# Decoding w_in in sixteen halves of 256 columns instead of eight parts of 512

## The chip, the core and the metric

The kernel runs on one core of a Trainium2 chip. TensorE (PE) multiplies, VectorE (DVE), ScalarE (ACT) and GpSimd (POOL) work on rows of up to 128 partitions, SyncE (SP) only issues transfers. Each engine takes its instructions strictly in the order of its own queue, and waits on semaphores for the other engines.

The metric is the device time of one execution in microseconds, the median of several runs; lower is better.

## The reference

The weights w_in, w_out, w_ch1 and w_ch2 come as 64-bit floats, the rest in single precision. The reference is one attention layer and two feed-forward layers, one behind the other:

```python
scores = scale * q @ k.T          # 4 batches, 8 heads, 576 positions, head width 64, block-causal mask
attn   = softmax(scores) @ v      # -> x: 4 x 576 x 512
h      = relu(x @ w_in)           # w_in: 512 x 1024; u = first half, v = second half
v_n    = (v - mean) / sqrt(var + 1e-6)
v_s    = w_spatial @ v_n + b_spatial
x      = (u * v_s) @ w_out
out    = x + relu(layernorm(x) * g_ln @ w_ch1) @ w_ch2
```

## The kernel before, in words

Attention runs over 16 pairs of heads, and each pair is cut into 9 **units** of query blocks (`UNITS`, line 249): one unit for the 64 rows left over in both heads, then for each head the blocks with 512, 384, 256 and 128 keys. A unit is a matmul of scores on PE, the row maximum and subtraction on DVE (L319), the exponential on ACT (L326), then transposes back on PE (L376), whose results DVE or ACT copies out of PSUM (L368, L370), and at the end of a pair the product with v (L427). The loop of line 557 writes these steps unit by unit; `u` counts the units, so pair p begins at unit 9p.

Matmuls here work on pairs (high, low) of single-precision numbers: `mm3` (L106 to L108) makes three products of them. Who makes such pairs from plain numbers is a `split`: one instruction rounds the value (high), a second subtracts (low). Queries and keys are split into `stack` (rounding on DVE or ACT, L56 and L58; subtraction on POOL, L227, L239, L241); the result of attention is scaled and split into `xT` on POOL (L437, L60, L440).

**w_in** arrives as raw 64-bit words, and `decode` (line 81) makes single-precision numbers of them in three instructions: ACT takes the high words (L88, tile `dm`), DVE shifts the low words (L89, tile `de`), and DVE joins both (L90). The split of w_in is all on POOL: L101 rounds `dm` into `win[0]`, L102 subtracts into `win[1]`. `decode_in` (line 443) does it for eight parts: four row blocks of the columns of v (parts 0 to 3), then four of those of u (parts 4 to 7). Three raw buffers take turns; `fetch(i + 3)` (L450, on the SP queue) loads a part into the buffer of part i once that is decoded. The first product with v's columns is a `value_tile`, the first with u's columns a `gate_unit` (tile `ups`); those of one batch are put in between the attention units of the next.

When the parts are decoded is set by `DECODE` (line 556), a set of units: the first one starts the loads, each further unit decodes one part. L88 and L89 are pinned to that place in the written order (`tc.keep_in_program_order`); all other instructions are put into each engine's order by a scheduler that works with modelled times. The tile `dm` shares a ring of three buffers (`vr`) with the value tiles, `de` a ring of two (`ur`).

Behind attention come the spatial product, w_out and the second feed-forward layer, with their own decodes of 128x256 tiles (`decode_jobs`, line 717); these are not touched.

Of the kernel before, what the change touches and what calls it, by code (L numbers as in the profile page):

```python
# [20 lines left out]
PLAN = {'mm': 3, 'sc': 3, 'tr': 2, 'D': 2, 'hi0': 'v', 'hi1': 's', 'klo0': 'g', 'klo1': 'g', 'qlo0': 'g', 'qlo1': 'g', 'xm0': 'g', 'xm1': 'g', 'xh0': 'g', 'xh1': 'g', 'xl0': 'g', 'xl1': 'g', 'dm': 'g', 'dh': 'g', 'ev0': 3, 'ev1': 2, 'rate': 24500.0, 'vrb': 3, 'ds': 2, 'dy': 1, 'raw': 5, 'yn': 2, 'ts': 3, 'ring': 8, 'wt': 2, 'cb': 1, 'hq': 8, 'packed': 4, 'plain': 3, 'pre': 8, 'py': 10, 'pyn': 4, 'dn0': 2, 'dnn': 5, 'vl': 'v', 'pace': 3, 'wd': 7, 'tl0': 'v', 'tl1': 'v', 'xe': 's', 'pt': 6, 'dstart': 8}  # L21


def f32(ap):
    return ap.bitcast(F32)
# [8 lines left out]
def tile_kernel(  # L34
# [29 lines left out]
    F = w_in.shape[2] // 2  # L64
# [16 lines left out]
    def decode(raw, m, e, out, here=lambda ins: ins):  # L81

        low, high = raw[:, :, 0], raw[:, :, 1]
        here(nc.scalar.activation(m, f32(high), AF.Prelu, scale=2.0**-112, alpha=2.0**32))  # L88
        here(nc.vector.tensor_scalar(e, low, 29, None, op0=ALU.logical_shift_right))  # L89
        nc.vector.scalar_tensor_tensor(  # L90
            out.bitcast(U32), m.bitcast(U32), 3, e, op0=ALU.logical_shift_left, op1=ALU.bitwise_or
        )

    def split(src, hi, lo, high="s", low="g"):

        if high == "s":
            nc.scalar.copy(hi, src)  # L97
        elif high == "v":
            nc.vector.tensor_copy(hi, src)
        else:  # L100
            nc.gpsimd.tensor_scalar(hi, src, 1.0, 0.0, op0=ALU.mult, op1=ALU.add)  # L101
        {"v": nc.vector, "g": nc.gpsimd}[low].tensor_tensor(lo, src, f32(hi), op=ALU.subtract)  # L102
# [29 lines left out]
    win = [xw.tile([128, KD, 2 * F], F32R, name=f"win{i}") for i in range(2)]  # L132
# [310 lines left out]
    def decode_in():  # L443
        raws = {}

        def fetch(i):
            if i < 2 * KD:
                h, kc = 1 - i // KD, i % KD
                raws[i] = dn.tile([128, F, 2], U32, tag="hl", name="raw", bufs=3)
                nc.sync.dma_start(  # L450
                    out=raws[i].rearrange("p a b -> p (a b)"), in_=wi32[:, kc, 2 * F * h:2 * F * h + 2 * F]
                )

        fetch(0)
        fetch(1)
        fetch(2)
        yield
        for i in range(2 * KD):
            h, kc = 1 - i // KD, i % KD
            m = dn.tile([128, F], F32, tag="vr", name="dm", bufs=PLAN["vrb"])  # L460
            e = dn.tile([128, F], U32, tag="ur", name="de")
            cols = slice(F * h, F * h + F)
            decode(raws.pop(i), m, e, m, tc.keep_in_program_order)
            split(m, win[0][:, kc, cols], win[1][:, kc, cols], PLAN['dh'])
            fetch(i + 3)
            yield

    def value_tile(pair, t):

# [54 lines left out]
    dense = None  # L524
    debt = 0.0
    dec = decode_in()
    preps = {}

# [24 lines left out]
    tot = float(sum(size) * NP)  # L553
    D = PLAN['D']
    WARM = {2: 5, 3: 2, 4: 2, 5: 1}
    DECODE = {1, 7, 12, 17, 22, 38, 42, 46, 50}
    for u in range(NS + 8):
        p, i = divmod(u, NU)
        if u < NS:
# [21 lines left out]
        if 0 in preps and i >= 1:  # L581
            next(preps[0], None)
        if u in DECODE:
            next(dec, None)
# [115 lines left out]
    raws = {}  # L700
# [485 lines left out]
```

## Time and profile before

| | us |
|---|---|
| median of 3 runs | 806.68 (804.15 to 809.35) |
| the profiled execution | 802.63 |
| its span in the trace | 800.5 |
| PE busy | 779.9 (97% of the span) |
| DVE, ACT, POOL busy | 528.8, 419.4, 414.4 |

The span is the time from the first to the last instruction in the trace; the time of an execution has 2.1 us more around it. PE is busy nearly throughout, so a change of time has to show as a change of PE's idle time, or as PE's first and last work coming at another time. The busy share of the other engines is a mean: in the attention stage, which takes the first 264 us, POOL is at times as full as PE. PE's granted clock is 1.00 of full speed (2.4 GHz) in every stretch read below.

### The profile page before, as it was taken

Reading aid. Unit: us, or ns where it says so; the run is one execution under the profiler, and the core shown is the slowest. Engines: PE = TensorE matmul, PEld = TensorE weight load, DVE = VectorE, ACT = ScalarE, POOL = GpSimd, SP = SyncE. Lnnn points to the kernel's source line nnn. Section 1 sums busy time; section 2 is a strip of 40 time slices with the busy share of each in tenths; the row PEclk is TensorE's granted clock in tenths of the full one; section 3 lists DMA queues with packets and bytes.
Section 4 is the critical chain, followed back from the end, with each engine's and each line's share of the span. In section 5 each row is a group of like instructions: output and inputs, shape, how many; then the busy total and the mean of one; then the engine's idle time right before and its main releaser. Section 6 shows DMA issues by size and latency. Waiting matters only on the chain.

```text
span 800.5 us, 13287 instructions
## 1 busy us (share of the span) xinstructions
PE 779.9 (97%) x4508; PEld 669.0 (84%) x4508; DVE 528.8 (66%) x1193; ACT 419.4 (52%) x1071; POOL 414.4 (52%) x417
## 2 busy tenths in 40 slices
PE   9989999999999999999999999999999999999998
PEld 4667788778878799889988889888889888888986
DVE  6667855674565277787677787897566588645534
ACT  4777666666755464555354555653354454333421
POOL 4498856754553343223285465465545465545431
PEclk9999999999999999999999999999999999999999
DMA  8855545446141569789420342204001003000002
GB/s 252 198 158 164 149 148 152 131 121 177 68 156 61 152 204 297 214 258 287 150 93 2 106 131 79 80 0 158 1 28 28 0 1 125 21 0 1 1 1 79
DMA packets 53847, 88.70 MB, mean 111 GB/s; under 512 B 6930, under 2 KB 17298, under 8 KB 53780
## 3 DMA queue, kind: packets, MB, share of 16 engines
q1 hardware_dynamic: 53540, 87.55, 36.1%
q8 instruction: 35, 0.57, 0.3%
q10 hardware_dynamic: 240, 0.31, 0.2%
q14 instruction: 32, 0.26, 0.1%
HBM read 68.88 MB, written 18.95 MB: 110 GB/s over the span
## 4 chain that ended last, share of the span: by engine, by line
PE 80%; DVE 6%; DMA 5%; POOL 3%; ACT 2%; issue 2%; SPq 1%; POOLq 0%; ACTq 0%; DVEq 0%
PE hps L965 21%; PE o L106 8%; PE o L108 8%; PE o L107 8%; PE tr L376 5%; PE pv L427 5%; PE sc L304 3%; DMA raw<-in_w_ch_dram 2%; PE ups L106 2%; PE sc L298 2%; PE by L106 2%; PE by L108 2%; PE by L107 2%; PE sc L282 1%; PE ups L108 1%
## 5 line engine op out<-in xcount | busy, mean ns | idle before, releaser
L102 POOL TENSOR_TENSOR a<-s,a 128x256 fp32r<-128x256 f32 x96 | 78.0, 816 | 93.2 <-ACT a L97 93.2
L107 PE MATMUL o<-w,h 128*128 128x512 f32 x288 | 113.0, 394 | 0.0
L106 PE MATMUL o<-w,h 128*128 128x512 f32 x288 | 107.9, 398 | 1.0 <-ACT h L957 1.0
L971 DVE TENSOR_TENSOR c<-hps,c 128x384 f32<-128x384 f32 x120 | 66.5, 554 | 54.8 <-PE hps L965 52.8
L108 PE MATMUL o<-w,h 128*128 128x512 f32 x288 | 97.6, 398 | 0.1
L326 ACT ACTIVATE p<-p,nm 128x512 f32<-128x512 f32 (+3 forms) x128 | 71.2, 557 | 32.0 <-DVE nm L319 26.6
L319 DVE CUSTOM_DVE_ANT_0 p<-sc,mask 128x512 f32<-128x512 f32 (+3 forms) x128 | 58.5, 479 | 40.6 <-PE sc L304 18.9
L102 POOL TENSOR_TENSOR a<-w,a 128x256 fp32r<-128x256 f32 x72 | 61.5, 856 | 44.3 <-ACT a L97 38.6
L97 ACT CAST a<-s 128x256 fp32r<-128x256 f32 x96 | 38.4, 404 | 84.0 <-PE hps L965 75.8
L368 DVE COPY pH<-tr 128x512 f32<-128x512 f32 (+1 forms) x88 | 49.7, 574 | 27.4 <-PE tr L376 26.4
L106 PEld LDWEIGHTS o<-w,h 128*128 128x128 f32 x288 | 53.8, 188 | 11.6 <-ACT h L957 2.3
L107 PEld LDWEIGHTS o<-w,h 128*128 128x128 f32 x288 | 54.2, 188 | 10.1
L108 PEld LDWEIGHTS o<-w,h 128*128 128x128 f32 x288 | 53.2, 188 | 8.8 <-DVE h L958 1.0
L376 PE MATMUL tr<-idn,p 128*128 128x128 f32 x320 | 55.1, 279 | 4.5 <-DVE pH L368 4.4
L815 POOL TENSOR_TENSOR gt<-gf,gt 128x576 fp32r<-128x576 f32 (+1 forms) x17 | 25.5, 1501 | 59.6 <-ACT gt L814 59.6
L239 POOL TENSOR_TENSOR stack<-qkt,stack 64x576 fp32r<-64x576 f32 x24 | 34.7, 1444 | 33.6 <-ACT stack L58 29.3
L376 PEld LDWEIGHTS tr<-idn,p 128*128 128x128 f32 x320 | 37.7, 140 | 14.5 <-DVE pH L368 6.6
L958 DVE SCALAR_TENSOR_TENSOR h<-c,h 128x384 fp32r<-128x384 f32 x72 | 45.9, 657 | 1.5 <-ACT h L957 1.5
L117 POOL TENSOR_TENSOR rs<-rs,nhalf 128x1 f32<-128x1 f32 x36 | 23.3, 649 | 44.9 <-DVE rs L116 44.6
L88 ACT ACTIVATE dm<-raw 128x256 f32<-128x256 f32 (+1 forms) x72 | 31.9, 462 | 27.2 <-DVE w L90 8.0
L437 POOL TENSOR_TENSOR xx<-xx,rb 128x576 f32<-128x576 f32 x16 | 22.7, 1420 | 42.2 <-DMA rb<-r_d 30.1
L304 PE MATMUL sc<-stack 128*128 128x512 f32 (+3 forms) x192 | 43.5, 340 | 0.8 <-DVE nm L319 0.5
(185 smaller groups left out, 2276.7 us busy)
## 6 DMA issues: line engine op xcount, KB each, us to landing
raw<-in_w_ch_dram SPq DMA_DIRECT2D x64, 256.0 KB
qkt<-in_qk_dram SPq DMA_DIRECT2D x110, 144.0 KB
vt<-in_v_dram SPq DMA_DIRECT2D x16, 320.0 KB
rb<-r_d SPq DMA_DIRECT2D x32, 144.0 KB
u_d<-ur SPq DMA_DIRECT2D x16, 288.0 KB
us<-u_d SPq DMA_DIRECT2D x16, 288.0 KB
y_d<-ys SPq DMA_DIRECT2D x18, 256.0 KB
yr<-y_d SPq DMA_DIRECT2D x18, 256.0 KB
```

The costliest lines, as they stand in the source:

```text
L102: {"v": nc.vector, "g": nc.gpsimd}[low].tensor_tensor(lo, src, f32(hi), op=ALU.subtract)
L106: MM(out_ps, lhsT=a[0], rhs=b[0], start=first, stop=False)
L107: MM(out_ps, lhsT=a[0], rhs=b[1], start=False, stop=False)
L108: MM(out_ps, lhsT=a[1], rhs=b[0], start=False, stop=last)
L304: MM(s_ps[:, :nn], lhsT=st[:, j, i, q], rhs=st[:, j, 2, 0:nn], start=(i == 0), stop=(i == 1))
L319: nc.vector.tensor_tensor_reduce(pt[:, o:o + n], s_ps[:, :n], m, -0.125, 3e38, ALU.add, ALU.min, nm[:, i:i + 1])
L326: nc.scalar.activation(pt[:, :n], pt[:, :n], AF.Exp, bias=nm[:, 0:1], scale=-1.0, accum_out=sm[:, col:col + 1])
L368: nc.vector.tensor_copy(out, src)
L376: nc.tensor.transpose(tr[:, o:o + 128], pt[:, 128 * kc:128 * kc + 128], idn)
L958: nc.vector.scalar_tensor_tensor(t[:, 1], src, 0.0, f32(t[:, 0]), op0=ALU.max, op1=ALU.subtract)
L965: MM(ps, lhsT=a[x], rhs=b[y], start=not more and kc == 0 and k == 0, stop=kc == KD // 2 - 1 and k == 2, skip_group_check=True,)
L971: nc.vector.tensor_tensor(out, ps, x, op=ALU.add)
```

## The change

Each part of w_in is decoded and split in two halves of 256 columns. The halves stand at two units in a row (the old unit and the next), the pins on L88 and L89 are put on each half, and the next part is fetched after the second half. The tiles `dm`, `de` and the raw buffer stay one per part.

```diff
-            cols = slice(F * h, F * h + F)
-            decode(raws.pop(i), m, e, m, tc.keep_in_program_order)
-            split(m, win[0][:, kc, cols], win[1][:, kc, cols], PLAN['dh'])
-            fetch(i + 3)
-            yield
+            raw = raws.pop(i)
+            for a in range(0, F, F // 2):
+                part = slice(a, a + F // 2)
+                cols = slice(F * h + a, F * h + a + F // 2)
+                decode(raw[:, part], m[:, part], e[:, part], m[:, part], tc.keep_in_program_order)
+                split(m[:, part], win[0][:, kc, cols], win[1][:, kc, cols], PLAN['dh'])
+                if a:
+                    fetch(i + 3)
+                yield
...
-    DECODE = {1, 7, 12, 17, 22, 38, 42, 46, 50}
+    DECODE = {1} | {u + a for u in (7, 12, 17, 22, 38, 42, 46, 50) for a in range(2)}
```

So there are 8 more instructions on ACT, 16 more on DVE, 16 more on POOL, and as many transfers as before. Beyond about 120 us of the span the order of all engines is what it was. What moved before that is seen at three places.

**Place one: DVE at the end of the third pair** (units 25 and 26 and the next pair's first units; `tail` is the unit of the 64 leftover rows, `sm` its sums, `nm` the row maxima). Before:

```order
L368 COPY pH<-tr 128x4x128
L89 TENSOR_SCALAR de<-raw 128x512
L319 ISA p,nm<-sc,mask 128x128
L319 ISA nm 128x1
L319 ISA tail,nm<-sc,mask 128x256
L319 ISA nm 128x1
L319 ISA tail,nm<-sc,mask 128x320
L319 ISA nm 128x1
L90 SCALAR_TENSOR_TENSOR dm<-dm,de 128x512
L336 TENSOR_SCALAR sm<-sm 128x9
L323 TENSOR_TENSOR nm<-nm 128x1
L319 ISA p,nm<-sc,mask 128x512
```

and with the change:

```order
L368 COPY pH<-tr 128x4x128
L89 TENSOR_SCALAR de<-raw 128x256
L319 ISA p,nm<-sc,mask 128x128
L319 ISA nm 128x1
L319 ISA tail,nm<-sc,mask 128x256
L319 ISA nm 128x1
L319 ISA tail,nm<-sc,mask 128x320
L319 ISA nm 128x1
L90 SCALAR_TENSOR_TENSOR dm<-dm,de 128x256 x2
L323 TENSOR_TENSOR nm<-nm 128x1
L336 TENSOR_SCALAR sm<-sm 128x9
L319 ISA p,nm<-sc,mask 128x512
```

One shift of half the size stands where the whole one stood (its other half went to an earlier place), both joins stand together where one stood, and L323 went ahead of L336.

**Place two: DVE two pairs later** (part 4 and now also the first half of part 5). Before:

```order
L368 COPY pH<-tr 128x2x64
L89 TENSOR_SCALAR de<-raw 128x512
L90 SCALAR_TENSOR_TENSOR dm<-dm,de 128x512
L368 COPY pH<-tr 128x4x128
L319 ISA p,nm<-sc,mask 128x128
L319 ISA nm 128x1
L368 COPY pH<-tr 128x4x128
L319 ISA p,nm<-sc,mask 128x128
L319 ISA nm 128x1
L319 ISA tail,nm<-sc,mask 128x256
```

and with the change:

```order
L368 COPY pH<-tr 128x2x64
L89 TENSOR_SCALAR de<-raw 128x256
L90 SCALAR_TENSOR_TENSOR dm<-dm,de 128x256
L368 COPY pH<-tr 128x4x128
L89 TENSOR_SCALAR de<-raw 128x256
L319 ISA p,nm<-sc,mask 128x128
L319 ISA nm 128x1
L89 TENSOR_SCALAR de<-raw 128x256
L368 COPY pH<-tr 128x4x128
L319 ISA p,nm<-sc,mask 128x128
L319 ISA nm 128x1
L319 ISA tail,nm<-sc,mask 128x256
```

Half the decode stands ahead of the first copy, two more shifts between the first and the second copy; two joins follow behind this piece, ahead of the next row of `tail`.

**Place three: POOL around the last parts** (`rs` belongs to the value tiles, `stack` to a coming pair). Before:

```order
L437 TENSOR_TENSOR xx<-xx,rb 128x576
L117 TENSOR_TENSOR rs<-rs,nhalf 128x1 x2
L60 TENSOR_SCALAR xT_84<-xx 128x576
L440 TENSOR_TENSOR xT_85<-xx,xT_84 128x576
L101 TENSOR_SCALAR win_82<-dm 128x512
L102 TENSOR_TENSOR win_83<-dm,win_82 128x512
L101 TENSOR_SCALAR win_82<-dm 128x512
L102 TENSOR_TENSOR win_83<-dm,win_82 128x512
L239 TENSOR_TENSOR stack_89<-qkt,stack_89 64x576
```

and with the change:

```order
L437 TENSOR_TENSOR xx<-xx,rb 128x576
L101 TENSOR_SCALAR win_82<-dm 128x256
L117 TENSOR_TENSOR rs<-rs,nhalf 128x1 x2
L60 TENSOR_SCALAR xT_84<-xx 128x576
L102 TENSOR_TENSOR win_83<-dm,win_82 128x256
L440 TENSOR_TENSOR xT_85<-xx,xT_84 128x576
L101 TENSOR_SCALAR win_82<-dm 128x256
L102 TENSOR_TENSOR win_83<-dm,win_82 128x256
L101 TENSOR_SCALAR win_82<-dm 128x256 x2
L102 TENSOR_TENSOR win_83<-dm,win_82 128x256 x2
L239 TENSOR_TENSOR stack_89<-qkt,stack_89 64x576
```

Between the last split of `xT` and the next `stack` stood two whole parts; now three halves stand there, and the fourth is put in among the work ahead of them.

## Rows read from the trace of the kernel before

**Rows 1.** By stretch: length, busy us of PE, PEld, DVE, ACT, POOL; clock; DMA.
```profile
20.00:40.00 20.00, 19.41 (x130) 12.82 (x130) 13.81 (x45) 15.65 (x50) 9.98 (x12) 1.00 0.83 198
40.00:53.00 13.00, 11.08 (x81) 7.59 (x81) 10.03 (x30) 9.09 (x26) 12.49 (x12) 1.00 0.49 148
...
69.00:83.00 14.00, 12.65 (x87) 9.82 (x86) 12.06 (x33) 10.04 (x32) 12.71 (x11) 1.00 0.64 189
83.00:105.00 22.00, 20.52 (x139) 16.56 (x138) 16.79 (x49) 15.41 (x38) 18.29 (x17) 1.00 0.42 125
```

**Rows 2.** PE's waits from 20 to 110 us: us in total, times, longest.
```profile
PE tr L376 <- DVE pH L368: 2.8, 5, 1.3
PE tr L376 <- ACT rr L341: 0.9, 1, 0.9
PE sc L298 <- DVE nm L319: 0.9, 1, 0.9
PE rps L339 <- ACT pL L370: 0.8, 1, 0.8
PE sc L304 <- DVE nm L319: 0.5, 1, 0.5
```

**Rows 3.** Chain that ended last, 40 to 106 us: start, us, what.
```profile
44.83 1.29 DVE de L89
...
69.71 1.68 DVE dm L90
...
93.71 1.91 DVE de L89 x2
```

**Rows 4.** POOL in order of time: start, us, instruction.
```profile
44.43 1.40 POOL L239 TENSOR_TENSOR stack<-qkt,stack 64x576 fp32r<-64x576 f32 x1
...
69.33 1.51 POOL L239 TENSOR_TENSOR stack<-qkt,stack 64x576 fp32r<-64x576 f32 x1 [1.84 <-ACT stack L58]
```

**Rows 5.** Groups by line and shape, whole parts: count, busy us, mean ns.
```profile
L90 DVE SCALAR_TENSOR_TENSOR dm<-dm,de 128x512 uint32<-128x512 uint32 x8 | 7.7, 957 | 1.5 <-ACT dm L88 1.4
L89 DVE TENSOR_SCALAR de<-raw 128x512 uint32<-128x512 uint32 x8 | 5.8, 732 | 0.0
L88 ACT ACTIVATE dm<-raw 128x512 f32<-128x512 f32 x8 | 5.3, 666 | 0.9 <-DMA vn_d<-vr 0.9
```

**Rows 6.** Instructions of one line, ns min/median/max, first and last start, shapes.
```profile
L89 DVE TENSOR_SCALAR raw<-raw x68: 276/289/1367, 277.6 to 509.3; 128x256 uint32<-128x256 uint32 x64, 128x512 uint32<-128x512 uint32 x4
L89 DVE TENSOR_SCALAR de<-raw x8: 414/493/1654, 21.3 to 95.2; 128x512 uint32<-128x512 uint32 x8
...
L90 DVE SCALAR_TENSOR_TENSOR w<-dm,raw x32: 405/418/1553, 302.5 to 372.1; 128x256 uint32<-128x256 uint32 x32
L90 DVE SCALAR_TENSOR_TENSOR dm<-dm,de x8: 677/852/1684, 22.8 to 97.0; 128x512 uint32<-128x512 uint32 x8
...
L102 POOL TENSOR_TENSOR a<-s,a x96: 725/739/1495, 401.6 to 773.9; 128x256 fp32r<-128x256 f32 x96
L102 POOL TENSOR_TENSOR win<-dm,win x8: 1266/1279/1578, 24.3 to 99.7; 128x512 fp32r<-128x512 f32 x8
...
L101 POOL TENSOR_SCALAR win<-dm x8: 610/620/627, 23.6 to 99.0; 128x512 fp32r<-128x512 f32 x8
...
L60 POOL TENSOR_SCALAR xT<-xx x16: 661/672/682, 37.7 to 272.5; 128x576 fp32r<-128x576 f32 x16
...
L88 ACT ACTIVATE dm<-raw 128x256 f32<-128x256 f32 x64 | 26.6, 436 | 26.2 <-DVE w L90 8.0 <-DMA raw<-in_w_ch_dram 5.8 <-DVE w2b L90 5.4
```

**Rows 7.** The last split of w_in on POOL, and PE's first product with it, by time.
```profile
99.72 1.28 POOL L102 TENSOR_TENSOR win<-dm,win 128x512 fp32r<-128x512 f32 x1
...
103.25 0.29 PE L108 MATMUL ups<-xT,win 128*128 128x288 f32 x1
```

**Rows 8.** The SP queue's waits from 0 to 110 us: us in total, times, longest.
```profile
SPq L155 <- POOL stack L241: 13.7, 4, 4.6
SPq L450 <- DVE de L89: 3.4, 1, 3.4
```

## The prediction, made before the changed kernel ran

> **What bounds the kernel now.** First the busy times by stretch [rows 1]. PE is the engine to look at: from 40 to 53 us it works 11.08 of 13.00 us, from 69 to 83 us 12.65 of 14.00. These two stretches, where it idles 1.92 and 1.35 us, are not empty elsewhere: POOL is busy 12.49 and 12.71 us there and DVE 10.03 and 12.06, while from 20 to 40 us POOL has half its time free and PE idles only 0.59 us. The clock is at full speed throughout, so what PE loses it loses by waiting.
>
> Then PE's own waits from 20 to 110 us [rows 2]: 5.9 us in nine waits, all for DVE's copies and row maxima or for ACT work that hangs on these. POOL and transfers are not among them. So the question is what makes DVE late. The chain of waits [rows 3] has three long pieces of this very decode in it: the shift L89 at 44.83 us (1.29 us), the join L90 at 69.71 (1.68) and two shifts at 93.71 (1.91).
>
> Then why these are long. A shift of 512 columns takes 414 ns at best and 732 in the mean, a join 677 and 957 [rows 5, 6]. In order of time the long ones lie beside a POOL subtraction: the shift at 44.8 us ends at 46.12, 0.29 us after POOL's L239 that began at 44.43 and took 1.40; the join at 69.71 ends at 71.39, 0.55 us after the one that began at 69.33 and took 1.51 [rows 3, 4]. DVE stood until POOL's instruction was over, and then ran for about its own time. So a decode instruction has two prices: its own time, and the rest of the POOL instruction that it meets. Over the 16 shifts and joins the second price is (732 - 414) x 8 + (957 - 677) x 8 = 4.8 us, 0.30 us each.
>
> **The change part by part.** What is *added* is a fixed cost per instruction, from medians of half-size forms that the later stages run [rows 5, 6]:
> - ACT, 8 more L88: 2 x 436 - 666 = 206 ns a part, 1.6 us.
> - DVE, 16 more: the shift 2 x 289 - 414 = 164 ns, the join 2 x 418 - 677 = 159 ns; 2.6 us.
> - POOL, 16 more: L102 2 x 739 - 1279 = 199 ns. L101 has no row at 256 columns; from 620 ns at 512 and 672 at 576 (L60, the same operation) I take 0.81 ns a column, so 412 ns, an estimate. Its bounds are half of 620 and all of it; the added cost is 0 to 620 ns a part, 204 taken. Together 3.2 us (1.6 to 6.6).
>
> ACT's 1.6 us lie beside idle time: it works 9.09 of 13 and 10.04 of 14 us in the tight stretches. If that cover went, exponentials would come up to 0.2 us later a part. POOL's 3.2 us would be hidden too, since PE waits for no POOL work [rows 2], with one narrow place: the last L102 of w_in ends at 101.00 us, and PE first reads that tile's last row block at 103.25 [rows 7]. That is 2.25 us of cover; with all 3.2 us in front of it PE would wait 1.0 us.
>
> No transfer is added, but each reload of the raw buffer (L450) now waits for the second half, and stands later in the SP queue. Behind it are loads of queries and keys, which on their own wait up to 4.6 us for POOL to free the buffer; L450's worst wait for a shift is 3.4 us [rows 8]. A reload that comes a unit later, some 1.8 us (144 units in the first 264 us), lies inside that. I cost it at nothing; without that cover the loads would be later by those 1.8 us.
>
> What costs time is the *second price* on DVE, which is charged per instruction, not per column. Between 40 and 53 us and from 69 to 83 us, by the order shown, DVE gets five decode instructions more than before: one join at place one; at place two and right behind it two halves of shifts and two of joins. Where POOL is nearly always busy each has to stand again. Bounds for one: nothing beside its own 0.16 us (the shortest of the whole shifts, 414 ns, met nothing), or one whole POOL subtraction, 1.40 us [rows 4]. I take the mean of the rows, 0.30: 5 x (0.16 + 0.30) = 2.3 us. DVE has 2.97 and 1.94 us of idle time in the two stretches, but PE's waits say that it is late at their critical points, so I pass all of it on. From 20 to 40 us DVE has 6.2 us free and the added halves cost nothing.
>
> The SBUF — State Buffer page of the Trainium skill, in "SBUF: two separate sides", says that GpSimd and the DVE instructions that run in a two-port mode or read two inputs from SBUF share a port pair as an exclusive lock: whoever starts first holds it for the whole instruction, and the other fully blocks. The two collisions above agree. By the lock alone each added instruction would meet a busy POOL with the share 12.6 of 13.5 and stand half a subtraction, 0.66 us; five would be 4.1 us instead of 2.3.
>
> What is *gained*: ahead of the copy at 71.39 us for which PE waits now stands a half join, 677 - 418 = 0.26 us shorter, and at 44.8 us a half shift, 414 - 289 = 0.13 us shorter; the pause for the rest of POOL's instruction stays. At place three POOL has three halves between the last `xT` and the next `stack` instead of two parts: 3 x (412 + 739) = 3.45 against 2 x (620 + 1279) = 3.80 us, 0.35 us less on a piece that lies in the chain. Together 0.74 us.
>
> **Sum:** 2.3 - 0.7 = +1.6 us. Against the profiled execution (802.63) that is 804.2; this lies 4.05 us under the median of the runs shown, so against the median the forecast is 806.68 + 1.6 = **808.3 us**, 0.2% slower. The bounds of the second price give 5 x 0.16 - 0.7 = +0.1 and 5 x 1.56 - 0.7 = +7.1.
>
> **The rivals.**
>
> *A gain.* The units of the softmax get in between the halves, and the two worst collisions don't come again. For it: the shift at 44.8 us is followed by a wait of 0.9 us, and the longest wait of PE, 1.3 us, is for the copy behind the join at 69.71 [rows 2, 3]. Against: both halves of the join stand together at place one. If those two waits go and the fixed cost is hidden: -2.2, with place three -2.6: 804.1 us. More is hardly there, since all that PE loses from 20 to 110 us is 5.9 us. This is a chance of 0.22.
>
> *No change.* At place one and at place three halves stand side by side again (two joins, two roundings and two subtractions on POOL), so they are a whole instruction in two pieces. With only the 0.8 us of fixed cost of five DVE instructions against the 0.7 gained: 806.8 us. Chance 0.24.
>
> *Much slower.* DVE gets through one such instruction per POOL instruction: after a block POOL starts its next subtraction at once, and the second half stands for all of that. Its place is the two stretches and the three shifts and three joins around 93 to 98 us, where two and two stood: seven added instructions at 1.56 us, 10.9, less 0.7: 816.9 us. It decides from six whole blocks on (6 x 1.56 - 0.7 = 8.7). For it: the piece at 93.71 us. Against: 0.30 us in the mean, not 1.40. Chance 0.06.
>
> **How the numbers follow.** My forecast, a loss of 0.5 to 7 us, has 0.48. One per cent is 8.1 us, about what a measurement of this kernel can tell from no change (its three runs differ by 5.2). A gain of that size would need more than all waits in the stretch: 0.01. A loss of that size is the third rival: 0.06. Within 1%: 0.93. The range reaches from the gain to the upper bound of the forecast, less a tail on each side: 803.5 to 813 us.
>
> **What the profile would show.** Half shifts near 289 ns at best and joins near 418, with means 0.2 to 0.4 us above; L102 near 739 ns. PE's waits from 20 to 110 us at 6 to 9 us instead of 5.9, again for DVE copies and maxima, at 45 to 53 and 69 to 78 us. The times beyond 120 us shifted as one piece. I am wrong if the means of the halves lie at their best times (then the first rival), if PE waits for POOL's `win` or `stack`, or if it waits more than 0.5 us at places that have no half near them.

## The result, and the profile after

The changed kernel takes 810.15 us in the median of 15 runs (806.93 to 813.35), the kernel before 805.21 in 15 runs beside it: a ratio of 1.0071 with a 95% interval of 1.0056 to 1.0085. It is slower by some 4.9 us, within 1%, as forecast in sign and in range; the forecast's +1.6 us was a third of it.

The head of the page after, with PE's line and the clock line of the 40 slices (tenths of full speed):

```profile
span 809.8 us, 13334 instructions
...
PE 787.4 (97%) x4508; PEld 673.0 (83%) x4508; DVE 532.3 (66%) x1209; ACT 420.3 (52%) x1079; POOL 415.0 (51%) x433
...
PEclk9979999999999999999999999999999999999999
```

The span is 9.3 us longer than before. The same 4508 matmuls are busy 787.4 us instead of 779.9: 7.5 of the 9.3 us are matmuls that took longer, and only 1.8 us are added idle time (22.4 against 20.6). The slowest of these matmuls stand where the clock line has its 7. The two executions are not equally typical. This one lies 1.5 us above the median of its kernel, with a mean granted clock of 0.990 where the 15 runs have 0.994 in the median; the profiled execution of before (802.63) lies 2.6 us under the 805.21 of its kernel, with a clock of 1.0. So the pages show where time goes, and the medians how much.

The stretches of [rows 1] after (length, busy us of PE, PEld, DVE, ACT, POOL, then the granted clock):

```profile
20.00:40.00 20.00, 18.77 (x130) 12.56 (x129) 16.35 (x51) 14.96 (x50) 11.62 (x16) 1.00 0.84 197
40.00:53.00 13.00, 12.71 (x66) 8.38 (x67) 8.23 (x25) 7.80 (x21) 12.25 (x16) 0.74 0.56 156
...
69.00:83.00 14.00, 10.72 (x70) 7.92 (x70) 11.46 (x29) 7.78 (x23) 9.79 (x10) 1.00 0.48 141
83.00:105.00 22.00, 21.83 (x142) 17.07 (x138) 17.90 (x55) 15.39 (x44) 17.24 (x20) 1.00 0.46 137
```

From 40 to 53 us PE is busier than before and yet gets through 66 matmuls instead of 81: the clock is 0.74. From 69 to 83 us the clock is full, and PE idles 3.28 us instead of 1.35. Both losses are in the one table, and only the clock column tells them apart.

The same view with stretches cut where the clock changes:

```profile
40.00:46.90 6.90, 6.85 (x28) 4.72 (x28) 2.13 (x7) 4.20 (x10) 6.51 (x8) 0.51 0.54 143
46.90:57.00 10.10, 9.09 (x63) 5.90 (x62) 8.07 (x28) 7.61 (x26) 8.96 (x12) 1.00 0.64 170
57.00:60.60 3.60, 3.60 (x16) 2.74 (x18) 0.28 (x1) 2.72 (x6) 2.71 (x3) 0.53 0.15 45
60.60:108.30 47.70, 42.42 (x282) 32.33 (x284) 37.23 (x112) 32.03 (x95) 36.04 (x38) 1.00 0.47 140
108.30:111.70 3.40, 3.40 (x19) 2.90 (x16) 0.78 (x6) 2.71 (x5) 2.35 (x2) 0.51 0.40 119
```

PE runs near the 1.2 GHz level in three stretches, 13.9 us together. As an example of what one matmul costs there, by groups of shape (count, busy us, mean ns), the transposes of the leftover rows from 40 to 46.9 us after:

```profile
L376 PE MATMUL tr<-idn,tail 128*128 128x128 f32 x5 | 1.5, 430 | 0.0
```

and the same five in the kernel before, at full clock:

```profile
L376 PE MATMUL tr<-idn,tail 128*128 128x128 f32 x5 | 0.9, 283 | 0.0
```

What PE did before the first fall, in order of time:

```profile
38.15 0.28 PE L339 MATMUL rps<-idn,sm 128*9 128x128 f32 x1 [0.38 <-ACT pL L370]
38.36 0.61 PE L298 MATMUL sc<-stack 64*128 64x256 f32 x3
...
40.05 0.59 PE L264 MATMUL sc<-const-float32-0.0 128*128 128x512 bf16 x1 [0.31 <-DVE nm L319]
```

Two short waits, 0.38 and 0.31 us, for ACT and DVE; at 40.05 us the matmuls are already slow (0.59 us, where this one took 0.38 to 0.39 in the kernel before). The second wait comes from a half of the change. POOL, then DVE, in order of time:

```profile
37.97 1.41 POOL L440 TENSOR_TENSOR xT<-xx,xT 128x576 fp32r<-128x576 f32 x1
```
```profile
38.47 1.19 DVE L90 SCALAR_TENSOR_TENSOR dm<-dm,de 128x256 uint32<-128x256 uint32 x1
39.58 0.41 DVE L319 CUSTOM_DVE_ANT_0 p<-sc,mask 128x256 f32<-128x256 f32 x1
```

A half join that takes 0.41 us at best takes 1.19 and ends 0.28 us after the subtraction; the row maximum behind it ends at 39.99, and PE begins at 40.05.

PE's waits, now from 20 to 125 us since the work comes later (us in total, times, longest). They are 8.8 us; before has 5.9 in this window as in that of [rows 2], and up to 110 us they are 7.4 after:

```profile
PE sc L304 <- DVE nm L319: 2.9, 4, 1.1
PE tr L376 <- DVE pH L368: 2.3, 5, 1.0
PE tr L376 <- ACT rr L341: 1.2, 1, 1.2
PE rps L339 <- ACT pL L370: 1.2, 2, 0.8
PE tr L376 <- ACT pL L370: 0.5, 1, 0.5
PE sc L282 <- DVE nm L319: 0.4, 1, 0.4
PE sc L264 <- DVE nm L319: 0.3, 1, 0.3
```

None is for POOL or a transfer. The decode by groups of shape, against [rows 5]:

```profile
L102 POOL TENSOR_TENSOR win<-dm,win 128x256 fp32r<-128x256 f32 x16 | 12.1, 768 | 0.5
L90 DVE SCALAR_TENSOR_TENSOR dm<-dm,de 128x256 uint32<-128x256 uint32 x16 | 9.7, 626 | 0.9 <-ACT dm L88 0.8
L89 DVE TENSOR_SCALAR de<-raw 128x256 uint32<-128x256 uint32 x16 | 8.9, 571 | 0.0
L88 ACT ACTIVATE dm<-raw 128x256 f32<-128x256 f32 x16 | 6.6, 431 | 0.4 <-DMA vn_d<-vr 0.4
L101 POOL TENSOR_SCALAR win<-dm 128x256 fp32r<-128x256 f32 x16 | 6.6, 418 | 11.0 <-DVE dm L90 10.9
```

A half shift takes 571 ns in the mean where a whole one took 732, a half join 626 where a whole one took 957. Shifts and joins keep DVE busy 18.6 us instead of 13.5. How that happens is seen at place two, first POOL and then DVE, in order of time:

```profile
75.72 1.42 POOL L241 TENSOR_TENSOR stack<-qkt,stack 64x576 fp32r<-64x576 f32 x1
...
77.90 1.42 POOL L239 TENSOR_TENSOR stack<-qkt,stack 64x576 fp32r<-64x576 f32 x1
79.39 1.47 POOL L241 TENSOR_TENSOR stack<-qkt,stack 64x576 fp32r<-64x576 f32 x1
```
```profile
75.93 1.36 DVE L89 TENSOR_SCALAR de<-raw 128x256 uint32<-128x256 uint32 x1
77.21 0.68 DVE L368 COPY pH<-tr 128x512 f32<-128x512 f32 x1
78.36 0.55 DVE L368 COPY pH<-tr 128x384 f32<-128x384 f32 x1
78.83 2.31 DVE L90 SCALAR_TENSOR_TENSOR dm<-dm,de 128x256 uint32<-128x256 uint32 x2
81.48 0.55 DVE L368 COPY pH<-tr 128x384 f32<-128x384 f32 x1
```

The shift at 75.93 ends at 77.29, 0.15 us after L241, and the copy for which PE waits comes behind it. The two joins at 78.83 take 2.31 us (0.77 and 1.62): the first ends 0.28 us after one POOL subtraction, the second 0.28 us after the next. In one piece they would, by the same reading, have stood once. PE waits five times between 75 and 82 us, 3.3 us in all.

### The profile page after: what moved, and what is told of

Read it like the earlier page. It is cut to its first block, busy times and chain, and to the rows that moved or that the text cites. A ratio compares the mean times of both kernels' runs of the same rounds, so it can differ in the third digit from the quotient of the medians.

```text
span 809.8 us, 13334 instructions
## 1 busy us (share of the span) xinstructions
PE 787.4 (97%) x4508; PEld 673.0 (83%) x4508; DVE 532.3 (66%) x1209; ACT 420.3 (52%) x1079; POOL 415.0 (51%) x433
## 4 chain that ended last, share of the span: by engine, by line
PE 80%; DVE 9%; DMA 4%; issue 2%; POOL 2%; ACT 2%; SPq 1%; ACTq 0%; POOLq 0%; DVEq 0%
PE hps L969 21%; PE o L106 8%; PE o L108 8%; PE o L107 8%; PE pv L427 5%; PE tr L376 5%; PE sc L304 3%; PE ups L106 2%; PE vps L106 2%; PE ups L107 2%; PE ups L108 2%; PE by L106 2%; PE by L108 2%; PE by L107 2%; PE vps L108 1%
## 5 line engine op out<-in xcount | busy, mean ns | idle before, releaser
L88 ACT ACTIVATE dm<-raw 128x256 f32<-128x256 f32 x80 | 33.2, 435 | 26.1 <-DVE w L90 7.5
L437 POOL TENSOR_TENSOR xx<-xx,rb 128x576 f32<-128x576 f32 x16 | 22.8, 1427 | 42.4 <-DMA rb<-r_d 30.7
```

## The experiments

The theory: a DVE instruction of the decode costs its own time and the rest of the POOL instruction that it meets; with twice as many instructions DVE is later for the softmax, TensorE waits, and its clock falls. The rivals: POOL's added work; the second half's later place; an accident of the scheduler; DVE's own time alone, without standing. One more, ACT's eight added instructions, has no run of its own. Differences are of medians against the kernel before on the same chip.

**e1, both halves at the old unit.**

```diff
-                if a:
-                    fetch(i + 3)
-                yield
+            fetch(i + 3)
+            yield
...
-    DECODE = {1} | {u + a for u in (7, 12, 17, 22, 38, 42, 46, 50) for a in range(2)}
+    DECODE = {1, 7, 12, 17, 22, 38, 42, 46, 50}
```

> Both halves of a part decoded at the part's old unit, everything else as in the change. Theory A (each added DVE instruction costs its own time and the rest of the POOL instruction that it meets; TensorE then waits and its clock falls): as many added instructions as in the change, so 3 to 7 us over before. Rival (the second half's later unit, with the later reload of the raw buffer, is what costs): 0 to 1 us over before.

Measured: 812.30 against 803.50 us, ratio 1.0106 (1.0093 to 1.0119). +8.8 us is more than the theory's 3 to 7; the later place is not the cost, it is milder than the old one.

**e2, POOL alone in halves.**

```diff
-            split(m, win[0][:, kc, cols], win[1][:, kc, cols], PLAN['dh'])
+            for a in range(0, F, F // 2):
+                ...
+                split(m[:, part], win[0][:, kc, half], win[1][:, kc, half], PLAN['dh'])
```

> Decode on ACT and DVE in whole parts at the old units; only POOL's rounding and subtraction in two halves. Theory A: DVE gets no added instruction, and shorter POOL instructions can only shorten what it waits for: -1 to +1 us against before. Rival (the 16 added POOL instructions, some 3 us, are what costs): +3 to +5 us.

Measured: 802.74 against 803.50 us, ratio 0.9988 (0.9974 to 1.0001): no cost. POOL's added instructions are not the cause. The whole shifts and joins met less here (545 and 761 ns instead of 732 and 957):

```profile
L90 DVE SCALAR_TENSOR_TENSOR dm<-dm,de 128x512 uint32<-128x512 uint32 x8 | 6.1, 761 | 1.5 <-ACT dm L88 1.3
...
L89 DVE TENSOR_SCALAR de<-raw 128x512 uint32<-128x512 uint32 x8 | 4.3, 545 | 0.0
```

**e3, ACT and DVE in halves, POOL in whole parts.**

```diff
-                cols = slice(F * h + a, F * h + a + F // 2)
...
-                split(m[:, part], win[0][:, kc, cols], win[1][:, kc, cols], PLAN['dh'])
                 if a:
+                    cols = slice(F * h, F * h + F)
+                    split(m, win[0][:, kc, cols], win[1][:, kc, cols], PLAN['dh'])
                     fetch(i + 3)
```

> ACT and DVE decode in halves at two units in a row, as in the change; POOL splits the whole part behind the second half. Theory A: all 16 added DVE instructions are there, +3 to +6 us against before. Rival (POOL's added instructions cost): 0 to +1 us.

Measured: 807.81 against 803.50 us, ratio 1.0057 (1.0039 to 1.0075). +4.3 us: with e2, the loss of the change is in the decode's halves on ACT and DVE; which of the two engines, this pair does not tell.

**e4, quarters of 128 columns, two at each of the two units.**

```diff
-            for a in range(0, F, F // 2):
+            for a in range(0, F, F // 4):
...
-                yield
+                if a % (F // 2):
+                    yield
```

> Four quarters of 128 columns per part, two at the old unit and two at the next. Theory A: 48 added DVE instructions instead of 16, so about three times the change's 4.9 us, 10 to 16 us over before. Rival (the loss is an accident of where the scheduler puts things, not a price per instruction): 2 to 7 us over before.

Measured: 815.26 against 803.50 us, ratio 1.0140 (1.0122 to 1.0157). +11.8 us, in the theory's range and out of the rival's. A quarter join still takes 511 ns, a quarter shift 425, near the halves' 626 and 571; the shifts and joins together 29.5 us:

```profile
L90 DVE SCALAR_TENSOR_TENSOR dm<-dm,de 128x128 uint32<-128x128 uint32 x32 | 16.1, 511 | 2.2 <-ACT dm L88 1.7
...
L89 DVE TENSOR_SCALAR de<-raw 128x128 uint32<-128x128 uint32 x32 | 13.4, 425 | 0.0
```

**e5 and e6, more matmuls by zero, in the change and in the kernel before.**

```diff
-    ZEROS = {9 * p + i: n for p in range(4) for i, n in ((8, 1), (9, 2))}
+    ZEROS = {9 * p + i: n for p in range(8) for i, n in ((8, 2), (9, 2))}
```

> The change, with 20 more of the matmuls by zero that already stand ahead of two units at each pair's end (2 and 2 for the first eight pairs instead of 1 and 2 for the first four): some 0.2 us of TensorE work each, 4.3 us. Theory (a good part of the loss is TensorE's clock falling to half after its own waits): the mean granted clock rises from 0.994 towards 0.998 and the change with zeros lies only 1.5 to 3.5 us over the kernel before with the same zeros. Rival (waits alone): the distance between the two stays at 4 to 6 us, whatever the clock shows.

> The kernel before with the same 20 matmuls by zero, as the other end of that comparison. Both theories: 0 to 4.3 us over before (nothing where TensorE would have waited, 0.2 us each where not); with the clock theory less than 3, since before too loses some clock (0.998).

Measured: the change with zeros 817.66, before with zeros 811.23, before 803.58 us. Both expectations failed. The zeros cost 7.7 us instead of at most 4.3, the clock did not rise (median 0.992 in the change with zeros, 0.996 in the other), and the distance of the two, 6.4 us, is even a little above the rival's 4 to 6. The zeros are written into the same tile as the scores behind them, so they can't start before that is free. They fill no idle time: PE idles 28.7 and 24.2 us in the two profiled executions, against 22.4 and 20.6 without them (up to 2 us of that are zeros whose records are missing). This pair says nothing for the clock's part; that rests on the rows above.

**e7 and e8, POOL's long subtractions cut in two, in the kernel before and in the change.**

```diff
-            nc.gpsimd.tensor_tensor(st[low, j, 0, :], raw[low, j, 0, :], ...)
+            for a in (0, HS):
+                c = slice(a, a + HS)
+                nc.gpsimd.tensor_tensor(st[low, j, 0, c], raw[low, j, 0, c], ...)
```

(and the same for the other half of the rows)

> The kernel before with POOL's subtractions L239 and L241 (1.42 us, 576 columns) cut into two of 288 columns, 48 more instructions on POOL at some 0.2 us. Theory (a DVE instruction stands for the rest of the POOL instruction that it meets): shifts and joins meet at most 0.8 us, their mean falls from 732 and 957 ns by 100 to 200 ns, and the time is -4 to 0 us against before. Rival (DVE waits for POOL as an engine, however its work is cut, and POOL's added time counts): 0 to +5 us.

> The change with the same cut of L239 and L241. Theory: the price per added DVE instruction halves, so the distance to the kernel before with that cut is 1 to 3 us instead of 4.9. Rival (the halves cost by their number and place alone): the distance stays at 4 to 6 us.

Measured: before with short subtractions 804.18 against 803.58 us, ratio 1.0006 (0.9987 to 1.0026); the change with them 807.43, ratio 1.0047 (1.0029 to 1.0066). The distance falls from 4.9 to 3.3 us: between the two expectations, nearer to the theory's 1 to 3, but each of the two ratios is uncertain by some 1.5 us, so a fall of 1.6 us is not clear of noise. In one execution of each, PE waits 5.6 us in e7 and 5.5 in e8 from 20 to 125 us, where the long subtractions have 5.9 and 8.8; that is for the theory, but is no more than one pair. And in e7 the mean of shifts and joins did not fall (760 and 1048 ns), as the theory had said it would. Two rows show how. A shift beside the short ones, and a join that met a subtraction of the scaled result (L437 of before), still whole; POOL and DVE, two pieces in order of time:

```profile
44.84 1.74 POOL L241 TENSOR_TENSOR stack<-qkt,stack 64x288 fp32r<-64x288 f32 x2
...
78.36 1.44 POOL L441 TENSOR_TENSOR xx<-xx,rb 128x576 f32<-128x576 f32 x1
```
```profile
45.26 0.67 DVE L89 TENSOR_SCALAR de<-raw 128x512 uint32<-128x512 uint32 x1
...
78.55 1.80 DVE L90 SCALAR_TENSOR_TENSOR dm<-dm,de 128x512 uint32<-128x512 uint32 x1
```

Between the short ones the shift took 0.67 us, 0.25 above its best, where the one of [rows 3] took 1.29, 0.88 above; the join took 1.80 us, 1.12 above its best, beside an instruction that had not been cut. In these two the block follows the rest of the one instruction that is met.

**e9 and e10, whole parts and 16 extra DVE instructions on a scratch tile of 192 columns** (a join with two inputs in SBUF, or a reciprocal).

```diff
+    EXTRA = {u + a for u in (7, 12, 17, 22, 38, 42, 46, 50) for a in range(2)}
...
+        if u in EXTRA:
+            tc.keep_in_program_order(nc.vector.scalar_tensor_tensor(
...
```

> The kernel before, whole parts, with 16 extra joins of 192 columns on a scratch tile (two inputs in SBUF, as L90), pinned at the 16 units of the change. Own time by the rows 677 - 320 x 1.0 = some 0.35 us each, an estimate; with the rest of POOL's instructions some 0.6. Theory (such an instruction costs its own time and the rest of the POOL instruction that it meets): 4 to 9 us over before. Rival (any DVE time counts alike): the same as the next run within 1.5 us.

> The kernel before with 16 extra reciprocals of 192 columns on the same scratch tile at the same places; the reciprocals of the trace (L337) took 0.20 us whether POOL was busy or not. Own time some 0.4 us each, an estimate. Theory: DVE is busy as long, but stands for nothing, so 0 to 3 us over before, and at least 3 us less than the run with joins. Rival: the same as that run within 1.5 us.

Measured: 814.70 with joins and 818.04 with reciprocals, against 803.22 us; ratios 1.0140 (1.0116 to 1.0164) and 1.0178 (1.0152 to 1.0204). Both theories missed. The reciprocal was a bad control: I had taken it for 0.4 us, and it took more than three times that (ns min/median/max):

```profile
L587 DVE RECIPROCAL scr<-scr x16: 1328/1342/1349, 16.5 to 109.1; 128x192 f32<-128x192 f32 x16
```
```profile
L587 DVE SCALAR_TENSOR_TENSOR scr<-scr,mask x16: 344/354/1568, 16.0 to 106.4; 128x192 uint32<-128x192 uint32 x16
```

So the two were not of equal length, and what they show is another thing. The reciprocals never stood for POOL (21 ns from shortest to longest) and yet cost 14.8 us, with 21.5 us of DVE time added. Standing for POOL is not needed for a loss: DVE time added at these places costs, without a single instruction more on ACT. The joins cost 11.5 us; they take 9.4 us (0.59 in the mean, as expected), and the kernel's own shifts and joins 14.6 instead of 13.5, so 10.5 are added.

**e11 and e12, two small row operations out of POOL's way, in the kernel before and in the change.**

```diff
-            nc.vector.tensor_tensor(nm[:, 0:1], nm[:, 0:1], nm[:, 1:2], op=ALU.min)
+            nc.vector.tensor_scalar(nm[:, 0:1], nm[:, 0:1], nm[:, 1:2], None, op0=ALU.min)
...
-        nc.vector.tensor_scalar(sm, sm, 1e-9, None, op0=ALU.add)
```

> The kernel before with two small DVE instructions per pair taken out of POOL's way: L323 (minimum of two columns) as an operation with a per-partition scalar, a form that took 0.12 to 0.17 us beside a busy POOL (L116), and the addition of 1e-9 to the sums (L336) left out, since a sum is at least 1 and the addition changes no bit of it. The two took 9.4 and 9.1 us over the attention stage, of which some 5 are their own. Theory: -2 to -8 us against before. Rival (their waits are hidden): -1 to +1 us.

> The change with the same two instructions taken out of POOL's way. Theory: the halves keep their price, so 3 to 7 us over the kernel before with that edit, and near or under before. Rival (the change's loss comes from these small instructions, which now follow the halves): within 1.5 us of the kernel before with that edit.

Measured: 801.95 against 803.22 us, ratio 0.9979 (0.9962 to 0.9995), and 806.04, ratio 1.0036 (1.0019 to 1.0054). The small operation stands no more; before and then e11:

```profile
L323 DVE TENSOR_TENSOR nm<-nm x16: 144/563/1403, 8.3 to 243.4; 128x1 f32<-128x1 f32 x16
```
```profile
L323 DVE TENSOR_SCALAR nm<-nm x16: 149/206/210, 8.1 to 240.6; 128x1 f32<-128x1 f32 x16
```

The gain of 1.3 us is just clear of noise, but below the expected 2 to 8. In the profiled executions DVE is busy 516.1 us instead of 528.8, so 12.7 us of DVE time, spread over the attention stage, bought 1.3: most of it was hidden. e12 is 4.1 us above e11, so the halves keep their price, as expected; it is not back at the kernel before, as I had thought it might be. e11 is the fastest version of the study, below both kernels.

## Why the prediction was right, and where it was too small

The table takes one profiled execution of each kernel: DVE's time for shifts and joins (with the extra instructions), PE's idle time (span less busy), and PE's busy time; then, over all runs, the median of the mean granted clock and the difference of median times from before.

| kernel | DVE, us | PE idle | PE busy | clock | time |
|---|---|---|---|---|---|
| before | 13.5 | 20.6 | 779.9 | 0.998 | |
| e2, POOL in halves | 10.4 | 21.2 | 782.8 | 0.998 | -0.8 |
| the change | 18.6 | 22.4 | 787.4 | 0.994 | +4.9 |
| e1, one unit | 20.5 | 23.6 | 784.9 | 0.991 | +8.8 |
| e3, decode in halves | 22.7 | 24.1 | 781.6 | 0.997 | +4.3 |
| e9, extra joins | 24.0 | 27.7 | 785.3 | 0.986 | +11.5 |
| e4, quarters | 29.5 | 26.7 | 787.7 | 0.992 | +11.8 |
| e10, reciprocals | 33.7 | 31.8 | 784.5 | 0.990 | +14.8 |

- *The second price* was right in the mean: 0.30 us per instruction forecast, (571 - 289 + 626 - 418) / 2 = 245 ns measured over all halves, and some 0.34 us over the eleven that start from 40 to 57 and from 69 to 84 us (six before, so the five added ones are as forecast). Their places are another thing: "the pause for the rest of POOL's instruction stays" failed, for the half shift and the half join at the two old places met nothing (0.29 us at 48.25, 0.42 at 73.36), and other halves met POOL instead. The lock of the Trainium skill's page SBUF — State Buffer ("SBUF: two separate sides"), taken with POOL's busy share, gave 0.66; the form of the collisions agrees with it, the size does not: this order of instructions met POOL less than that.
- *The own times* were right: half shifts and joins at 276 and 413 ns at best, L101 at 418 where I estimated 412.
- *POOL* cost nothing, as said: PE waited for none of its work, and e2 shows it. *ACT and the transfers* are not shown to cost nothing. PE's waits behind ACT rose from 1.7 to 2.9 us, which can be ACT's eight instructions or the DVE work ahead of it. PE waited for no load; but a load of `qkt` stands for 2.17 us, from 103.97 us on, in the chain that ended last, ahead of PE's wait of 1.2 us at 107 us, and before has no load in its chain from 20 to 110 us.
- *The waits* were forecast at 6 to 9 us instead of 5.9; they are 7.4 in the forecast's window and 8.8 up to 125 us. The sum's +1.6 us is to be held against +1.5 to +2.9 for them, in an execution that idles 1.8 us more over its whole span.
- *A term put at nothing* was not nothing: "From 20 to 40 us DVE has 6.2 us free and the added halves cost nothing". There DVE works 16.35 us instead of 13.81 [rows 1], and PE idles 1.23 instead of 0.59. The mean of DVE's idle time did not help where a half join stood right ahead of a row maximum, at 38.47 us; the first fall of the clock follows that wait.
- *What failed* most is a sentence of the first part, "the clock is at full speed throughout, so what PE loses it loses by waiting". I took the clock of the kernel before for a given. In the profiled execution after, PE is busy 7.5 us longer with the same matmuls, and 13.9 us of the span run near 1.2 GHz. This term was missing from the sum. In the 15 runs the clock is between 0.989 (813.35 us) and 0.998 (807.81); a straight line through all runs of the study, with a level of its own for each kernel, gives 0.55 us per 0.001 (give or take 0.05). The median clock is 0.994 after and 0.998 for the runs of before whose clock is known, so some 2 us of the 4.9 are the clock and the rest waits. That is an estimate, since those runs of before are from the other comparisons. By the same line some 3 us are left at equal clock of e3's 4.3, and as much of the 4.1 between e12 and e11. e3's profiled execution comes nearest to a test of this: its clock is 0.998, its PE busy time 1.7 us above before and its idle time 3.5.
- *The rivals.* "No change" is out by the interval. "A gain" is out by the sign: the two old collisions did go, as it said, but others came, the shift at 75.93 and the joins at 78.83. "Much slower" is in the wrong size: not seven whole blocks.

What stays open: what exactly makes the clock fall. Waits of 0.38 and 0.31 us came before the fall at 40 us, while longer ones, 1.0 and 1.1 us between 77 and 82 us, were followed by none, and before had one of 1.3 us at full clock. No experiment held the clock. Nor is it settled why e1 costs twice what e3 does with less DVE time: by the line above some 3 of the 4.5 us between them go with the clock, and why that falls more in e1 is the same question. The table's order holds only roughly, and the place of each instruction counts beside their sum. How much of the loss is standing, and how much the instructions' own time, is read from rows alone, since the pair e9 and e10 did not part them; and ACT's added instructions were not run by themselves.

## What to carry to other kernels

Cutting an instruction in two pays only if what waits behind it can get in between and if the pieces are not charged per instruction; on an engine that stands for another's instructions each piece pays that charge again. When DVE feeds TensorE closely, count what is added to DVE right ahead of the work that TensorE waits for, also in a stretch where DVE has idle time in the mean; time far from there can be free, as e11 shows. Then allow for TensorE's granted clock: cost it from a profile that has both levels, not from one that shows only the full one.

## What was not expected of the hardware

- TensorE ran at 0.51 to 0.53 of its clock in three stretches of 3.4 to 6.9 us although it was busy nearly all of them, and after waits of no more than 1.2 us each; a transpose of 128 columns took 430 instead of 283 ns.
- A reciprocal of 192 columns on DVE took 1.34 us against 0.35 for a join, and never stood for POOL.
- A minimum of two columns took 144 to 1403 ns as an operation of two tensors, and 149 to 210 with a per-partition scalar.
